# One more second product by two Strassen levels in a fused attention and expert kernel

## The chip, the cores and the metric

The kernel runs on one core of one Trainium2 chip. The metric is device time in microseconds (us) of one execution; smaller is better. The core has a matrix engine (TensorE, PE in the profile), three engines for elementwise work (VectorE or DVE, ScalarE or ACT, GpSimd or POOL), and a queue engine (SyncE, SP) that issues nearly all DMA transfers here. Every engine works through its own instructions in order and waits on semaphores for the others. PEld is TensorE's weight load, which overlaps its matmuls.

## The reference

First comes a linear attention with decay over blocks of 64 tokens (4 batches, 8 heads, 768 tokens, head size 64). Its output, brought to 3072 rows of 512, is the input `x` of four expert networks, whose results are added with normalised weights:

```python
x = np.ascontiguousarray(attn_out.transpose(0, 2, 1, 3)).reshape(B * S, H * D)   # 3072 x 512
p = domain_probs / (domain_probs.sum(-1, keepdims=True) + 1e-09)
for e in range(4):
    h = np.maximum(x @ w1[e], 0.0)          # 512 x 1024
    out += p[:, e:e + 1] * (h @ w2[e])      # 1024 x 512
```

Everything is float32. In this document `x @ w1[e]` is the first product and `h @ w2[e]` the second one.

## The kernel before, in words

The 3072 tokens are cut into three groups g of 1024. A pair (g, e) of a group and an expert is a unit; there are twelve, numbered 0 to 11 in the order in which they are worked. Strassen's scheme replaces the eight products of 2x2 blocks by seven, at the price of sums of blocks before and after. The first products of units 1 to 11 use it on two levels (7 x 7 block products). The second products of groups 0 and 1 (units 0 to 7) use it on one level: seven products `M1` to `M7`, each made of sixteen 128x128x256 matmuls (`second_product`, matmuls at L1028). Those of group 2 (units 8 to 11) use two levels: 7 x 7 products of two such matmuls each (`nested_product`, L1256). So a one-level second product costs 112 matmuls and a two-level one 98. The profile records each of these float32 matmuls as two instructions. The last unit has a few special forms (`plain_product`, `turned_product`).

The second product of unit u and the first product of unit u+1 are interleaved by the main loop: seven products, each in eight slots. After every slot the loop advances its own clock `now[0]` by one and hands out other work: queued VectorE sums (`background`), GpSimd steps (`aside`), the attention of the next groups, and `pump`, which starts larger GpSimd jobs from the list `chores` and the DMA stores from `queue` by due times. Those due times come from a rough cost model in the same units (`busy` for GpSimd, `filled` for VectorE, `free` for when the next chore may begin). In each engine the instructions stand in the order that this gives.

One-level form. The hidden blocks are turned into operand sums by VectorE (`operands`, `later_operands`), tokens are the rows of the result, and `scalar_tensor_tensor` at L1046 multiplies with the token's gate and adds into eight `acc` tiles, which SP stores straight to the output after expert 3.

Two-level form. GpSimd first multiplies the hidden blocks with the gates (`gated`, with `gate_bc`, which lies in the `decay` tile of the attention), VectorE and ScalarE make the outer sums T1 to T4 (`outer_sums`: ScalarE copies one operand to PSUM as `hp` at L838, VectorE writes `hT`), GpSimd makes the inner sums into `acc` tiles (`inner_sums`), and the results pile up in seven `sums` tiles in which the rows are output columns and the columns are tokens. They are added over the four experts and turned only once, at the end. The `sums` tiles take all seven buffers of the pool `stage`.

The two-level form needs each w2 block split into seven operands (S and A blocks) in DRAM, `w2_ops`. `prepare_w2_ops(e)` makes them on GpSimd, one expert in each of units 4 to 7; it needs `stage` buffers too, and every operand set is written by six DMA stores. `feed3` reads them back as `w2t`, four loads for each product. `feed` loads w1 operands as `ws_in` with two buffers, each one product ahead. `x_fill` loads the x blocks of a group, and `x_inner` makes four differences from each of the seven on GpSimd (`xs`).

Line L102 is the helper `tt` through which all elementwise sums go, so the rows of the profile have to be told apart by tile names.

Of the kernel before, what the change touches and what calls it, by code (L numbers as in the profile page):

```python
# [21 lines left out]
def kernel(  # L22
# [78 lines left out]
    def tt(eng, o, a, b, op):  # L101
        eng.tensor_tensor(out=o, in0=a, in1=b, op=op)  # L102
        if eng is nc.gpsimd:
            busy[0] = max(busy[0], now[0]) + math.prod(o.shape[1:]) / 480
        else:
            vector(math.prod(o.shape[1:]), PSUM in (a.space, b.space))
# [6 lines left out]
    now, busy, free, filled = [0], [0.0], [0.0], [0.0]  # L113
# [7 lines left out]
    LAST = NG - 1  # L121

# [47 lines left out]
    def store(f):  # L170
        queue.append((busy[0] + 2, f))
# [7 lines left out]
    def pump(pace=1.0, force=False):  # L179
        all_added(None if force else now[0])  # L180
        while results:
            results.pop(0)()
        while late and (force or late[0][0] <= now[0]):
            late.pop(0)[1]()
        begins = chores and (force or free[0] <= now[0])
        while queue and (force or queue[0][0] <= now[0] or begins and len(queue) > LEFT):
            queue.pop(0)[1]()
        if begins:
            begin = free[0] = max(free[0], now[0] - 1)
            was = max(busy[0], now[0])  # L190
            chores.pop(0)()
            free[0] = max(free[0], begin + max(pace * (busy[0] - was), 1))
# [106 lines left out]
    def inner_w2(e, m, blk):  # L299
        b = {f"A{i + 1}{j + 1}": blk[:, j, :, i * P:(i + 1) * P] for i in range(2) for j in range(2)}  # L300
        s = stage.tile([P, 4, 2, P], FP32, name="ops", tag="st")
        for name, x, y, op in S_OPS:
            b[name] = s[:, SLOT[name]]
            tt(nc.gpsimd, b[name], b[x], b[y], op)
        to = w2_ops[e, MS.index(m)]
        store(lambda: (
            nc.sync.dma_start(out=to[:, 0], in_=b["A11"]),
            nc.sync.dma_start(out=to[:, 1:3], in_=s[:, 0:2]),
            nc.sync.dma_start(out=to[:, 3], in_=b["A22"]),
            nc.sync.dma_start(out=to[:, 4], in_=b["S1"]),  # L310
            nc.sync.dma_start(out=to[:, 5], in_=b["A12"]),
            nc.sync.dma_start(out=to[:, 6], in_=b["S4"]),
            made.add(("w2", e, m)),
        ))

    def prepare_w2_ops(e):
        st = {}

        def block(name, i, j):
            t = stage.tile([P, 2, 2, DH], FP32, name="w2b", tag="st")  # L320
            src = moe_w2[e, j * W:(j + 1) * W, i * DH:(i + 1) * DH]
            nc.sync.dma_start(out=t[:].rearrange("p q c d -> p (q c) d"), in_=src.rearrange("(k p) d -> p k d", p=P))
            st[name] = t

        def total(name, a, b, op):
            t = stage.tile([P, 2, 2, DH], FP32, name="w2o", tag="st")
            halves(*(x[:].rearrange("p q c d -> p q (c d)") for x in (t, st[a], st[b])), op)
            st[name] = t

        return weight_steps(block, total, lambda m: inner_w2(e, m, st[A_OF[m]]))  # L330
# [21 lines left out]
    def x_fill(g, m):  # L352
# [8 lines left out]
        chores.insert(0, lambda: x_inner(g, m))  # L361
# [133 lines left out]
    last_gate = consts.tile([P, CPG * E], FP32, name="last_gate")  # L495


    gate_rows = dram.tile([CPG, E, P], FP32, name="gate_rows")
    gate_bc = decay[:]

    def gates():
# [8 lines left out]
        for i in range(CPG):  # L510
            t = token(LAST, i // 4, i % 4) // P
            nc.vector.tensor_copy(out=last_gate[:, i * E:(i + 1) * E], in_=gate[:, t])

    def turn_gates():
        p, o = bank("s0", "gp"), small("gr")
        n = CPG * E
        nc.tensor.transpose(out=p[0:n, 0:P], in_=last_gate[:], identity=ident[:])
        nc.scalar.copy(out=o[0:n, 0:P], in_=p[0:n, 0:P])
        nc.scalar.dma_start(out=gate_rows[:].rearrange("n e p -> (n e) p"), in_=o[0:n, 0:P])
# [291 lines left out]
    outer = {e: {n: {} for n in ("B11", "B12", "B21", "B22", "T1", "T2", "T3", "T4")} for e in range(E)}  # L811
# [43 lines left out]
    EARLY = E - 1, "M3"  # L855
# [42 lines left out]
    def finished(g, e, m, blocks, new):  # L898

        def later(to, a, b, order, relu=False):  # L900
# [7 lines left out]
            def step(at):  # L908
                x = there[at]
                if g == LAST and at != order[-1]:  # L910
                    bring(order[order.index(at) + 1])
                o = to[at] if at in to else small("m" + at)
                tt(nc.vector, o[:], x[:], b[at][:], ALU.add)
                if relu:
                    nc.scalar.activation(out=o[:], in_=o[:], func=AF.Relu)  # L915
                    if g == LAST:
                        gated(e, 1, 1, at, o)
# [4 lines left out]
            if g == LAST:  # L922
# [3 lines left out]
        def keep(c, i, j):  # L926
            if g == LAST:
                outer_sums(e, *{(0, 1): (("T1",), ("T3", "T2")), (1, 0): (("T4",),)}.get((i, j), ()))
# [21 lines left out]
    def first_product(g, e, m, blocks, tags):  # L950
# [3 lines left out]
        while (g, e) == (0, 1) and to_do[m]:  # L954
# [12 lines left out]
        def inner(i):  # L967
# [17 lines left out]
            if m in OUT and (at == "12" or not begins):  # L985
                nc.scalar.activation(out=new[at][:], in_=new[at][:], func=AF.Relu)  # L986
                if g == LAST:
                    gated(e, *OUT[m], at, new[at])
# [24 lines left out]
    def second_product(g, e, m, banks):  # L1013

        def part(sj, s):
# [31 lines left out]
            if e == E - 1 and m in ("M2", "M6", "M5", "M3"):  # L1047
                results.append(lambda: nc.sync.dma_start(out=rows[n][:, j * DH:(j + 1) * DH], in_=o))
# [10 lines left out]

    SEQ3 = ("M1", "M3", "M5", "M7", "M6", "M2", "M4")  # L1060
# [3 lines left out]
    def feed3(e, m, k):  # L1064

        until(("w2", e, m))
        if e == E - 1 and m != SEQ3[0]:

            if k == 0:
                t = xp.tile([P, 7, 256], FP32, name="w2s", tag="x" + SEQ[SEQ3.index(m)])  # L1070
                if (e, m) == PLAIN:
                    i, j = int(A_OF[m][1]) - 1, int(A_OF[m][2]) - 1
                    src = moe_w2[e, j * W:(j + 1) * W, i * DH:(i + 1) * DH]
# [3 lines left out]
                nc.sync.dma_start(out=t[:], in_=w2_ops[e, MS.index(m)].rearrange("p k c d -> p k (c d)"))  # L1077
# [6 lines left out]
            out=t[:, 0:n], in_=w2_ops[e, MS.index(m), :, 2 * k:2 * k + n].rearrange("p k c d -> p k (c d)"),  # L1084
# [97 lines left out]
    PLAIN = E - 1, "M2"  # L1182
# [23 lines left out]
    END = E - 1, SEQ3[-1]  # L1206
# [28 lines left out]

    def nested_product(e, m, tags):
        if e == 0:
# [8 lines left out]
        def inner(x, i):  # L1246
# [16 lines left out]
            if begins and e == 0:  # L1263
# [7 lines left out]
        def done():  # L1271
            if e == E - 1:
                to_join(m)

# [13 lines left out]
    def own_x(m):  # L1288
# [3 lines left out]
        def sub(f):  # L1292
            def step():
                steps.pop()
                f()
                if not steps:
                    made.add(("x", 0, m))
# [3 lines left out]
        for f in x_steps(0, m, nc.vector):  # L1301
            sub(f)
        own_sums.extend(steps)
# [149 lines left out]
    units = [(g, e) for g in range(NG) for e in range(E)]  # L1453
    fill = [(*u, m) for u in units[2:] for m in SEQ]
    fill2 = [(*u, m) for u in units[:-E] for m in SEQ2]
# [51 lines left out]
    fill3 = [(e, m, k) for e in range(E) for m in SEQ3 for k in range(4)]  # L1507
# [6 lines left out]
    PACE = 1.0, 1.4, 1.0  # L1514
    for at, (g, e) in enumerate(units):
# [3 lines left out]
        nested, nests = g == LAST, ahead and ahead[0] == LAST  # L1519
        if g == LAST - 1:  # L1520
            chores.extend(prepare_w2_ops(e))
        if at == 6:
            forget()
        blocks, banks = {}, {}
        for i in range(7):
            if fill2:
                feed2(*fill2.pop(0))
            if (g, e) < (LAST, 0):
# [5 lines left out]
            if nests and i == 2:  # L1534
                nc.scalar.dma_start(
                    out=gate_bc, in_=gate_rows[:, ahead[1]].partition_broadcast(P),
                )
            if nested:
                pair = (at * 7 + i) % 2 if ahead else i % 3
                b = nested_product(e, SEQ3[i], (("q01", "q02"), ("q11", "q12"), ("g1", "g3"))[pair])  # L1540
                if i < 6 and (e, SEQ3[i + 1]) != PLAIN:
                    inner_sums(e, SEQ3[i + 1])
            else:
                b = second_product(g, e, SEQ2[i], banks)
            if nests and i == 6:
                inner_sums(ahead[1], SEQ3[0], nested)
                if ahead[1] == EARLY[0]:
# [4 lines left out]
            if nested and (e, SEQ3[i]) == END:  # L1552
# [9 lines left out]
            for x, part in enumerate(order):  # L1562
# [15 lines left out]
                if nested or nests:  # L1578
                    take(aside)
                if nested and ahead and x in (1, 3) and fill3:  # L1580
# [47 lines left out]
```

## Time and profile before

| | |
|---|---|
| median of 3 runs | 1175.31 us (1172.42 to 1177.07) |
| the profiled execution, its own time | 1171.55 us |
| its span, from first to last instruction | 1169.8 us |
| TensorE busy | 1157.8 us, 99% of the span |
| VectorE, GpSimd, ScalarE busy | 791.7, 646.1, 271.1 us |
| moved by DMA | 255.63 MB |
| unit 7: from its first second-product matmul to that of unit 8 | 772.77 to 864.73 us |
| unit 8: the same | 864.73 to 949.41 us |

A row of the groups names the line, engine and operation, then "out<-in" by tile names, the shapes, "xcount", the busy time with the mean of one in ns, and last the idle time of the engine before these instructions with what ended it. A waits row reads "engine, line, waited for: total us, times, longest". A row of the stretches gives, for a window, its length and for each engine the busy us and the number of instructions, then the granted TensorE clock, the DMA share and GB/s. A timeline row has start, length, engine, line, operation and count.

### The profile page before, as it was taken

The numbers are of one execution on the slowest core, as the hardware profiler recorded it, in microseconds if no ns is written. First come the engines' busy times: TensorE is split into PE (matmuls) and PEld (weight loads), VectorE is DVE, ScalarE is ACT, GpSimd is POOL, SyncE is SP. The second block draws the span as 40 slices with busy tenths as digits, with TensorE's granted clock in tenths as the row PEclk, the third lists the DMA queues.
The fourth block names the chain that finished last, engine by engine and source line by source line (L and its number), as shares of the span: only waits on it lengthen the run. The fifth ranks groups of instructions, "written<-read, shape, count | busy, mean of one in ns | idle before, by whom it ended". The sixth has DMA issues, their size and how long they took to land.

```text
span 1169.8 us, 21185 instructions
## 1 busy us (share of the span) xinstructions
PE 1157.8 (99%) x8095; PEld 1006.5 (86%) x8095; DVE 791.7 (68%) x1407; ACT 271.1 (23%) x540; POOL 646.1 (55%) x640
## 2 busy tenths in 40 slices
PE   8999999999999999999999999999999999999998
PEld 7888888888888888888888888888888888888887
DVE  4666895578478567657747836745775666777785
ACT  4321122112211201211211120221233342341231
POOL 2846327546655761065245215655893683882884
PEclk9999999999999999999999999999999999999999
DMA  9884668998997996787868757785765445354442
GB/s 208 219 257 153 185 195 264 289 315 255 310 334 228 311 277 188 221 264 230 247 195 261 243 182 239 215 278 184 252 212 194 140 152 181 129 182 148 154 180 73
DMA packets 265717, 255.63 MB, mean 219 GB/s; under 512 B 121328, under 2 KB 219408, under 8 KB 265616
## 3 DMA queue, kind: packets, MB, share of 16 engines
q1 hardware_dynamic: 254976, 251.46, 69.0%
q10 hardware_dynamic: 10640, 2.82, 1.1%
q8 instruction: 64, 1.05, 0.4%
q14 instruction: 37, 0.30, 0.1%
HBM read 180.80 MB, written 77.61 MB: 221 GB/s over the span
## 4 chain that ended last, share of the span: by engine, by line
PE 95%; DVE 3%; POOL 1%; issue 0%; DMA 0%; ACTq 0%; ACT 0%; POOLq 0%; DVEq 0%
PE pg L974 39%; PE q L1028 31%; PE pq L1256 13%; PE pM L1358 2%; PE pc L1358 2%; DVE m L102 1%; PE sp L633 1%; PE op L687 1%; PE op L705 1%; PE sp L640 1%; PE qp L603 1%; PE kp L603 1%; POOL acc L102 1%; POOL m L102 1%; DVE sums L102 0%
## 5 line engine op out<-in xcount | busy, mean ns | idle before, releaser
L974 PE MATMUL pg<-xs,ws_in 128*128 128x256 f32 x1960 | 471.6, 380 | 0.8 <-DVE m L102 0.7
L1028 PE MATMUL q<-w2t,m 128*128 128x256 f32 x1792 | 424.4, 380 | 0.0
L974 PEld LDWEIGHTS pg<-xs,ws_in 128*128 128x128 f32 x1960 | 369.8, 190 | 53.7 <-DVE m L102 3.3
L102 DVE TENSOR_TENSOR m<-pg,m 128x512 f32<-128x512 f32 x451 | 307.2, 687 | 120.0 <-PE pg L974 109.8
L1028 PEld LDWEIGHTS q<-w2t,m 128*128 128x128 f32 x1792 | 339.3, 190 | 46.6 <-DVE m L102 0.4
L1046 DVE SCALAR_TENSOR_TENSOR acc<-q,gate,acc 128x256 f32<-128x256 f32 x192 | 92.3, 481 | 126.2 <-PE q L1028 125.7
L102 DVE TENSOR_TENSOR m<-m,m 128x512 f32<-128x512 f32 x184 | 152.5, 829 | 7.7 <-ACT m L986 7.7
L986 ACT ACTIVATE m<-m 128x512 f32<-128x512 f32 x132 | 83.0, 630 | 303.6 <-DVE m L102 302.5
L102 POOL TENSOR_TENSOR m<-m,decay 128x512 f32<-128x512 f32 x64 | 81.8, 1293 | 58.1 <-ACT m L986 44.7
L102 DVE TENSOR_TENSOR sums<-pq,sums 128x256 f32<-128x256 f32 x153 | 64.1, 421 | 45.7 <-PE pq L1256 36.9
L982 ACT COPY m<-pg 128x512 f32<-128x512 f32 x88 | 51.5, 585 | 186.1 <-PE pg L974 176.1
L1256 PE MATMUL pq<-acc,w2t 128*128 128x256 f32 x352 | 86.6, 379 | 0.0
L102 POOL TENSOR_TENSOR xs<-xs 128x256 f32<-128x256 f32 x56 | 44.5, 794 | 73.1 <-DMA xs<-x_blocks 57.4
L1256 PEld LDWEIGHTS pq<-acc,w2t 128*128 128x128 f32 x352 | 66.8, 190 | 9.3 <-issue 0.3
L102 POOL TENSOR_TENSOR to<-xc 128x256 f32<-128x256 f32 x16 | 12.5, 783 | 95.8 <-DVE xc L102 67.8
L102 POOL TENSOR_TENSOR acc<-hT,hT 128x512 f32<-128x512 f32 x32 | 40.2, 1269 | 29.7 <-PE pq L1256 27.8
L102 POOL TENSOR_TENSOR kn<-kn,decay 128x512 f32<-128x512 f32 x16 | 18.0, 1123 | 64.6 <-PE kp L603 43.7
L102 POOL TENSOR_TENSOR w2o<-w2b 128x512 f32<-128x512 f32 x32 | 42.4, 1348 | 18.3 <-DMA w2b<-in_moe_w_dram 10.2
L915 ACT ACTIVATE m<-m 128x512 f32<-128x512 f32 x44 | 27.7, 630 | 106.8 <-DVE m L102 106.8
L102 POOL TENSOR_TENSOR ops<-w2b 128x256 f32<-128x256 f32 x24 | 17.8, 764 | 50.7 <-issue 28.2
L102 POOL TENSOR_TENSOR acc<-hT,acc 128x512 f32<-128x512 f32 x32 | 40.7, 1271 | 7.4 <-PE pq L1256 5.4
L102 POOL TENSOR_TENSOR w2o<-w2b,w2o 128x512 f32<-128x512 f32 x24 | 34.2, 1449 | 5.8 <-issue 4.3
(135 smaller groups left out, 1204.8 us busy)
## 6 DMA issues: line engine op xcount, KB each, us to landing
ws_in<-w_ops SPq DMA_DIRECT2D x70, 896.0 KB, 6.3
w2t<-w_ops SPq DMA_DIRECT2D x66, 256.0 KB, 5.1
w2t<-w_sums SPq DMA_DIRECT2D x64, 256.0 KB, 3.7
w_ops<-ops SPq DMA_DIRECT2D x28, 512.0 KB, 4.3
w2t<-in_moe_w_dram SPq DMA_DIRECT2D x48, 256.0 KB, 3.6
w2b<-in_moe_w_dram SPq DMA_DIRECT2D x32, 256.0 KB, 5.5
w_sums<-w2o SPq DMA_DIRECT2D x16, 512.0 KB, 5.7
w2b<-in_moe_w_dram SPq DMA_DIRECT2D x16, 512.0 KB, 7.6
```

Of the source, the lines that this page charges most:

```text
L102: eng.tensor_tensor(out=o, in0=a, in1=b, op=op)
L603: nc.tensor.transpose(out=x[:, ac * C:(ac + 1) * C], in_=y[:, 2 * ac:2 * ac + 2].rearrange("p r d -> p (r d)"), identity=ident[:],)
L633: nc.tensor.matmul(out=sp[r][half[x], ac * BL:(ac + 1) * BL], lhsT=hc(kT)[half[r], ac, blk[x]], rhs=hc(qT)[half[r], ac, blk[x]], start=(ac ...
L640: nc.tensor.matmul(out=sp[x][half[r], 256 + ac * D:256 + (ac + 1) * D], lhsT=kd[half[x], 2 * ac + r], rhs=vn[half[x], 4 * r + ac], start=F ...
L915: nc.scalar.activation(out=o[:], in_=o[:], func=AF.Relu)
L974: nc.tensor.matmul(out=p[:, j * 256:(j + 1) * 256], lhsT=ws[i][:, j * P:(j + 1) * P], rhs=xs[i], start=(fresh and j == 0), stop=True, skip ...
L982: nc.scalar.copy(out=new[at][:], in_=p[:])
L986: nc.scalar.activation(out=new[at][:], in_=new[at][:], func=AF.Relu)
L1028: nc.tensor.matmul(out=p[:, s * DH:(s + 1) * DH], lhsT=h[A_OF[m]][:, c * 256 + s * P:c * 256 + (s + 1) * P], rhs=fed2[g, e, m][uu][:, c], ...
L1046: nc.vector.scalar_tensor_tensor(out=o, in0=x, scalar=w, in1=o, op0=ALU.mult, op1=ALU.add)
L1256: nc.tensor.matmul(out=p[:, 0:256], lhsT=fed3[e, m, x // 2][:, x % 2, c * P:(c + 1) * P], rhs=b[B_OF[i]][:, c * 256:(c + 1) * 256], start= ...
L1358: nc.tensor.matmul(out=p[:, s * 256:(s + 1) * 256], lhsT=a[c][:, f:f + P], rhs=b[:, c, j * 256:(j + 1) * 256], start=(s == 0 and c == 0 an ...
```

## The change

Unit 7, which is group 1 with expert 3, now makes its second product in the two-level form. What goes with it:

- The last group works its experts in the order 3, 0, 1, 2; units 7 and 8 both read the w2 operands of expert 3.
- The operands of experts 3, 0 and 1 are queued together at unit 4 (`PREPARED`); those of expert 2 are made from unit 7 on, with tiles of the general pool, since the seven `stage` buffers now hold `sums` from unit 7 on. From then on (`spare`) GpSimd chores start at least 8 slots apart and only when GpSimd is modelled as free, and stores fall due 8 slots after the modelled end.
- Experts 0 to 2 of group 1 still end in `acc` tiles, which are stored to a DRAM tile `partial` in unit 6. The two-level result of unit 7 is joined by VectorE and GpSimd (`first_done`), parked in DRAM (`parked`, columns by tokens), gathered in eight tiles of 128 tokens as 32x32 blocks (four DMAs each), turned by VectorE's 32x32 transpose, added to `partial` by GpSimd and stored.
- For four of the seven x blocks of group 2 the four differences go to VectorE.
- The gates of group 1 are turned as well, and `gate_bc` is written from unit 6 on.

```diff
-            busy[0] = max(busy[0], now[0]) + math.prod(o.shape[1:]) / 480
+            busy[0] = max(busy[0], now[0]) + math.prod(o.shape[1:]) / (640 if spare else 480)
...
+    units = [(g, e) for g in range(NG) for e in ((3, 0, 1, 2) if g == LAST else range(E))]
+    unit_of = {u: x for x, u in enumerate(units)}
+    NEST = 2 * E - 1
+    FINAL = len(units) - 1
...
-        queue.append((busy[0] + 2, f))
+        queue.append((busy[0] + (8 if spare else 2), f))
...
-        begins = chores and (force or free[0] <= now[0])
+        begins = chores and (force or free[0] <= now[0] and not (spare and busy[0] > now[0] + 1))
...
-            free[0] = max(free[0], begin + max(pace * (busy[0] - was), 1))
+            free[0] = max(free[0], begin + max(pace * (busy[0] - was), 8 if spare else 1))
...
+        return [
+            lambda: (block("A21", 1, 0), block("A22", 1, 1)), pause(6),
+            lambda: total("S1", "A21", "A22", ALU.add),
+            lambda: (ready("M4"), block("A11", 0, 0), drop("A22")), pause(4),
+            less, lambda: ready("M7"), lambda: (ready("M1"), drop("S3")), lambda: ready("M5"),
+            lambda: (total("S2", "S1", "A11", ALU.subtract), block("A12", 0, 1)), lambda: ready("M6"),
+            lambda: ready("M2"),
+            lambda: total("S4", "A12", "S2", ALU.subtract), lambda: ready("M3"),
+        ]
...
-        chores.insert(0, lambda: x_inner(g, m))
+        if g == LAST and SEQ.index(m) >= 3:
+            own_x(m, g, 6)
+        else:
+            chores.insert(0, lambda: x_inner(g, m))
...
-        for i in range(CPG):
-            t = token(LAST, i // 4, i % 4) // P
+        for i in range(LAST * CPG):
+            t = token(1 + i // CPG, i % CPG // 4, i % 4) // P
             nc.vector.tensor_copy(out=last_gate[:, i * E:(i + 1) * E], in_=gate[:, t])
...
-            if e == E - 1 and m in ("M2", "M6", "M5", "M3"):
-                results.append(lambda: nc.sync.dma_start(out=rows[n][:, j * DH:(j + 1) * DH], in_=o))
+            if unit_of[g, e] in (E - 1, NEST - 1) and m in ("M2", "M6", "M5", "M3"):
+                to = rows[n] if g == 0 else partial[n % CPG * P:(n % CPG + 1) * P]
+                results.append(lambda: nc.sync.dma_start(out=to[:, j * DH:(j + 1) * DH], in_=o))
...
+    def first_done(m):
...
+        def park(x):
+            i, j = RESULT[x]
+            to = parked[i * DH:(i + 1) * DH, j * W:(j + 1) * W].rearrange("(k p) t -> p k t", k=2)
+            of_x = of[x]
+            store(lambda: nc.sync.dma_start(out=to, in_=of_x[:].rearrange("p (k t) c -> p k (t c)", k=2)))
+
+        def gather(n):
+            t, po = small("y"), small("po")
+            for b in range(4):
+                c = n * P + b * 32
+                nc.sync.dma_start(
+                    out=t[b * 32:(b + 1) * 32].rearrange("p (r c) -> p r c", c=32),
+                    in_=parked[:, c:c + 32].rearrange("(r p) c -> p r c", p=32),
+                )
+            nc.sync.dma_start(out=po[:], in_=partial[n * P:(n + 1) * P])
+            gathered_out[n] = t, po
+
+        def turn_rows(n):
+            t = gathered_out[n][0]
+            nc.vector.transpose(out=t[:], in_=t[:])
+            vector(W, False)
+
+        def finish_rows(n):
+            t, po = gathered_out.pop(n)
+            tt(nc.gpsimd, t[:], t[:], po[:], ALU.add)
+            store(lambda: nc.sync.dma_start(out=rows[CPG + n], in_=t[:]))
...
+        if m == "M5":
+            for k in range(2):
+                then(1, ("M3", "M5"), lambda k=k: plus("M3", "M5", k, nc.gpsimd))
+        if m == "M6":
+            for a, b in (("M6", "M1"), ("M3", "M6"), ("M7", "M6"), ("M5", "M7")):
+                for k in range(2):
+                    then(1, (a, b), lambda a=a, b=b, k=k: plus(a, b, k))
+                if a in ("M3", "M5"):
+                    then(1, (a,), lambda a=a: park(a))
+        if m == "M2":
+            for k in range(2):
+                then(1, ("M1", "M2"), lambda k=k: plus("M2", "M1", k))
+            then(1, ("M2",), lambda: park("M2"))
+        if m == "M4":
+            for k in range(2):
+                then(1, ("M4", "M7"), lambda k=k: plus("M4", "M7", k))
+            then(1, ("M4",), lambda: park("M4"))
+            order = 4, 5, 6, 7, 0, 1, 2, 3
+            for n in order:
+                then(6, (), lambda n=n: gather(n))
+                then(6, (), lambda n=n: turn_rows(n))
+                then(2, (), lambda n=n: finish_rows(n))
...
-        if e == 0:
+        if e in (NEST, 2 * E):
+            while any(m in of for of, *_ in ending):
+                end_first(True)
             sums[m] = stage.tile([P, 4, 256], FP32, name="sums", tag="st")
...
-    fill2 = [(*u, m) for u in units[:-E] for m in SEQ2]
+    fill2 = [(*u, m) for u in units[:NEST] for m in SEQ2]
...
+    PREPARED = {NEST - 3: (3, 0, 1), NEST: (2,)}
...
-        nested, nests = g == LAST, ahead and ahead[0] == LAST
-        if g == LAST - 1:
-            chores.extend(prepare_w2_ops(e))
+        nested, nests = at >= NEST, ahead and at + 1 >= NEST
+        if at in PREPARED:
+            for x in PREPARED[at]:
+                chores.extend(prepare_w2_ops(x, nested))
+        if at == NEST:
+            spare.append(True)
...
+                    if own_sums and fits():
+                        take(own_sums)
+                if ending and fits():
+                    end_first()
```

## The prediction

> **What bounds the kernel now.** I read the page first (shares, groups), then the PE timeline for the true pace, then the stretches of single units, then the waits.
>
> ```profile
> span 1169.8 us, 21185 instructions
> PE 1157.8 (99%) x8095; PEld 1006.5 (86%) x8095; DVE 791.7 (68%) x1407; ACT 271.1 (23%) x540; POOL 646.1 (55%) x640
> ...
> L974 PE MATMUL pg<-xs,ws_in 128*128 128x256 f32 x1960 | 471.6, 380 | 0.8 <-DVE m L102 0.7
> L1028 PE MATMUL q<-w2t,m 128*128 128x256 f32 x1792 | 424.4, 380 | 0.0
> ```
>
> TensorE is busy 99% of the span, and before its two large groups it sat idle 0.8 and 0.0 us. So the number of matmuls sets the time, and other engines matter only where they would make TensorE wait. The 380 ns are not the pace, because matmuls overlap; the timeline has it:
>
> ```profile
> 772.77 1.89 PE L1028 MATMUL q<-w2t,m 128*128 128x256 f32 x8
> 774.50 1.89 PE L974 MATMUL pg<-xs,ws_in 128*128 128x256 f32 x8
> 776.22 1.89 PE L1028 MATMUL q<-w2t,m 128*128 128x256 f32 x8
> ```
>
> From start to start 16 records take 3.45 us: 215.7 ns each, and 215.9 over longer stretches. A matmul is two records, 0.432 us. The stretches of units 6 to 10:
>
> ```profile
> 682.00:772.80 90.80, 90.80 (x422) 79.75 (x421) 58.36 (x93) 14.74 (x24) 51.77 (x60) 1.00 0.73 230
> 772.80:864.70 91.90, 91.32 (x421) 79.42 (x420) 59.03 (x93) 21.17 (x36) 59.20 (x59) 1.00 0.74 239
> 864.70:949.40 84.70, 84.67 (x392) 74.58 (x393) 50.65 (x86) 33.58 (x72) 56.56 (x46) 1.00 0.49 165
> 949.40:1034.10 84.70, 84.70 (x394) 74.41 (x393) 61.73 (x114) 25.57 (x46) 55.29 (x45) 1.00 0.46 159
> ```
>
> A one-level unit has 420 records (90.7 us by the pace), a two-level one 392 (84.6 us). Unit 7 (second row) takes 1.3 us more than its records. The reason is a chain that starts on POOL:
>
> ```profile
> ACT hp L838 <- POOL m L102: 7.2, 1, 7.2
> ```
>
> ScalarE's first `hp` copy waited for a gated block, VectorE's `hT` behind it stood 1.97 us, and TensorE lost some 0.5 us, then another 0.67 us at the first two-level matmul, whose bank VectorE freed late. This is how a late GpSimd reaches TensorE.
>
> **The change, part by part.**
>
> *TensorE.* 14 matmuls fewer (112 to 98): 28 records x 215.9 ns = 6.05 us, all on the path. The transpose of the gates grows from 32 to 64 columns once, nothing.
>
> *VectorE* (rows: `acc` 481 ns, `m<-m,m` 829, `sums<-pq` 421, `hT` 681, `m<-up` 680, `xs` 653, transpose of 128x512 700). Removed: 28 `acc` steps (13.5 us) and 24 `m<-m,m` (19.9). Added: 21 `sums` additions (8.8), 16 `hT` (10.9), 8 `m<-up` (5.4), 12 joins of `sums` of which two operands lie in SBUF (taken as `m<-m,m`, 9.9), 16 `xs` differences (10.4), 8 transposes (5.6). Net +17.6 us over units 6 to 10, where the engine has 23 to 34 us free in each unit of 85 to 92; by the order of instructions unit 7 gets the most, about 66 us of work in 84.6. Hidden, so nothing, as long as no single lump is longer than what TensorE tolerates: by the timeline a bank is written again about 2.6 us after its last block ended, which leaves VectorE 1.9 us beside the 0.69 of its addition. The longest lump is three joins in a row at the start of unit 8 (2.5 us): I allow 0.3 us. The gates of group 1 add eight copies of 128x4 near 69 us (eight took 0.66 us); VectorE idles 1.04 us just after, so nothing.
>
> [...] `m<-m,m` takes 829 ns and single ones up to 1.45 us, against 687 with one operand in PSUM. [...] By the rows, which were taken beside a GpSimd 60 to 70% busy, unit 7 stays at 66. I take the rows.
>
> *GpSimd.* +54 sums of 128x512 (16 gate multiplications, 28 inner sums, 2 joins, 8 final additions; 1.27 us each, 68.6) and 16 `xs` fewer (x 0.79 = 12.7): +55.9 us. The w2 operands (28 small sums at about 0.79 and 8 at about 1.35, 33 us an expert) stay the same work but leave unit 6 and fill units 4 and 5; expert 2's fall into units 7 to 9. By order unit 8 then holds 43 gate and inner sums (54.6), two final additions (2.5), 20 small and 2 large operand sums (18.5): 75.6 of 84.6 us, after 56.6 before. Unit 9 holds 73, unit 10 52. So it is no bound on average, but 90% busy in order. Who waits? First TensorE for inner sums:
>
> ```profile
> 940.50 2.50 POOL L102 TENSOR_TENSOR acc<-m,m 128x512 f32<-128x512 f32 x2
> 943.09 2.63 POOL L102 TENSOR_TENSOR acc<-m,acc 128x512 f32<-128x512 f32 x2
> ...
> 952.93 1.89 PE L1256 MATMUL pq<-acc,w2t 128*128 128x256 f32 x8
> ```
>
> The last of these four ends at 945.72 and is first read at 953.79, 8.1 us later, which is the least margin in units 8 to 10. A chore ahead of it (4 small sums, 3.2 us) and a final addition (1.3) leave 3.6. Second, the `hp` copies, with almost no margin: adding up GpSimd's work in order puts five gated blocks some 2.4 to 3.4 us behind the place of the copy; the case above was about 6 us late and cost 0.5 us. I take 0.1 us each, 0.5 in all; at unit 7's old price it is 2.5.
>
> *ScalarE.* +28 copies of 128x256 (368 ns) and 20 of 128x512 (588): 22 us on an engine that is 23% busy. Nothing.
>
> *SP and DMA.* 82 issues more: 32 gathers, 8 loads of `partial`, 8 stores of rows, 4 of `parked`, the rest from operands that now come in halves. Moved: the stores to `partial` and the three operand sets pass SP one to three units sooner. Queued behind each are the next `w2t` and `ws_in`. The margins from landing to first use in units 8 to 10: `w2t` 3.6 us at the least and 6.5 as a rule, `ws_in` 6 to 9. SP runs ahead and then stands for TensorE:
>
> ```profile
> SPq L887 <- PE pg L974: 124.6, 19, 6.6
> ```
>
> That is 6.6 us in nearly every product of 12.1 us, room for ten issues of 0.6. A tile's gather is 2048 pieces of 128 bytes. No row has it; the nearest is `across`, 256 such pieces, 5.1 us to landing (2.1 to 9.9). A packet takes 50.6 ns of a DMA engine on average (69.0% of 16 x 1169.8 us over 254976 packets), so 2048 on 16 engines take 6.5 us, plus 2.1: some 9 us, at the upper end 8 x 3.0 + 2.1 = 26. The transpose stands at least 6 slots (9.1 us) behind, and SP issues ahead of its place. I take nothing, at 26 us it is rival three. Stores of GpSimd's results now come 8 slots later, so SP waits less for them.
>
> *Gone again:* unit 7's 1.3 us. The same first gating now lies in unit 6, where GpSimd has 44 instructions after 62 in the old place. I count two thirds, 0.9.
>
> **The sum.** -6.05 - 0.9 + 0.3 + 0.5 = -6.1 us. Span 1169.8 to 1163.7; the profiled execution, 1.75 us longer than its span, 1171.55 to 1165.4. It lies 3.8 us below the median of the runs, so the same step from the median gives 1169.2. A measurement of this kernel tells about 0.5% (5.9 us) from no change: the forecast lies just past that line, at 0.52%.
>
> **The rivals.**
>
> 1. *GpSimd falls behind.* For it: 90% in unit 8, the five late blocks, and its own model counts a small sum as 0.4 slots (0.6 us) where the rows have 0.79. Against: 8 us of margin on the inner sums. If each of the five costs 0.5 us and each two-level unit once meets a late inner sum (1 us for 3 units), +5 instead of +0.5: about 1172.5 (1170.5 to 1175).
>
> 2. *More than the matmuls is won.* All of unit 7's 1.3 us goes and nothing new comes: -7.3, 1168.0.
>
> 3. *The gathers hold up the weights: slower.* If eight gathers keep the DMA engines near the 26 us, the next `w2t` lands late by what exceeds 6.5 us of margin and the 9 us above. It decides from about 17 us a tile on; at 18.5 each of eight tiles costs 1.5 to 2 us, 12 to 16 in all: 1182. [...] Against: the DMA engines are only 46 to 50% busy in these units, and the 6.5 us from the packet's mean is taken from a mix with 121328 packets under 512 bytes.
>
> That the change does not do what it says can be left out: built, it has 2462 matmuls of 128x256 instead of 2476.
>
> **How the numbers follow.** The forecast with its own range of 1167 to 1170.8: 0.52; rival 2, 0.12; rival 1, 0.28; rival 3, 0.08. Faster by over 0.5% (under 1169.4): 0.38 of the first, 0.11 of rival 2 and 0.06 of rival 1, 0.55. Slower: rival 3 and a tail of rival 1, 0.08. The same: 0.37. The range reaches from rival 2's place less a us of scatter to the top of rival 1: 1166.8 to 1175.
>
> **What would show it.** Unit 7's stretch falls from 91.95 to about 84.8 us, units 8 to 10 stay at 84.7 to 85.5. GpSimd reaches about 75 us in unit 8. The `hp` copies show five or so waits for POOL of 2 to 4 us. The gathers land in 6 to 12 us. Wrong would be: units 8 to 10 over 86 us with TensorE idle before L1366 (inner sums, `w2t`), or transposes of `y` that wait for DMA with TensorE idle after them.

## The result

The changed kernel takes 1168.35 us in the median of 22 runs (1167.22 to 1175.77), the kernel before, over as many runs, 1175.83 us (1169.76 to 1183.16). The ratio of the means is 0.9945 with a 95% interval of 0.9928 to 0.9961: 0.55% faster, forecast 0.52%. The total came out as forecast; several of the terms in it did not, as the units show.

The page of the changed kernel, the lines that answer to those of before:

```profile
span 1169.7 us, 21473 instructions
PE 1155.8 (99%) x8067; PEld 1004.1 (86%) x8067; DVE 808.3 (69%) x1444; ACT 290.6 (25%) x588; POOL 702.8 (60%) x678
...
L1009 PE MATMUL pg<-xs,ws_in 128*128 128x256 f32 x1960 | 471.8, 381 | 1.2 <-DVE m L102 1.1
...
L1063 PE MATMUL q<-w2t,m 128*128 128x256 f32 x1568 | 371.3, 380 | 0.0
...
L1366 PE MATMUL pq<-acc,w2t 128*128 128x256 f32 x464 | 114.2, 379 | 0.6 <-DMA w2t<-w_ops 0.6
```

The group of one-level matmuls has lost 224 records, a unit's worth, and the largest two-level group now has an idle time of its own, 0.6 us before `w2t`. The span is the same as before, 1169.7 us, and that says nothing of the change: in this profile the part before unit 0 took 91.58 us, in that of before 86.40. From unit 0's first second-product matmul to the end it is 1078.13 us after 1083.36. The stretches of units 5 to 9, with the boundaries taken from this trace (columns as in the stretches of before):

```profile
590.70:687.20 96.50, 96.07 (x645) 83.47 (x645) 65.94 (x109) 16.23 (x32) 56.51 (x60) 1.00 0.76 239
687.20:777.90 90.70, 90.70 (x421) 79.71 (x420) 60.20 (x96) 21.04 (x36) 48.52 (x46) 1.00 0.69 218
777.90:862.90 85.00, 84.94 (x393) 74.23 (x392) 63.96 (x106) 33.08 (x71) 67.64 (x54) 1.00 0.60 200
862.90:949.20 86.30, 85.35 (x393) 74.22 (x392) 57.16 (x94) 34.62 (x74) 74.96 (x69) 1.00 0.83 254
949.20:1033.90 84.70, 84.70 (x393) 74.41 (x393) 63.28 (x117) 25.57 (x46) 64.77 (x54) 1.00 0.66 205
```

Unit 7 (third row) went from 91.96 to 85.0 us, as forecast, and no engine beside TensorE is full: GpSimd does 74.96 us of work in unit 8, forecast 75.6. But unit 8 costs 86.3 instead of 84.7, and unit 5 96.5 instead of 95.8. In unit 8 TensorE's timeline (start, length, instruction; in brackets the wait before it) says why:

```profile
907.28 1.10 PE L1366 MATMUL pq<-acc,w2t 128*128 128x256 f32 x4 [0.56 <-DMA w2t<-w_ops]
...
912.87 1.13 PE L1366 MATMUL pq<-hT,w2t 128*128 128x256 f32 x4 [0.18 <-DMA w2t<-w_ops]
```

By the starts of the matmuls the two waits cost 0.80 and 0.44 us. SP's own timeline of the 17 us before shows what the weights stood behind:

```profile
890.02 5.75 SPq L1300 DMA_DIRECT2D y<-parked  x4
898.52 0.34 SPq L1304 DMA_DIRECT2D po<-partial  x1
898.91 0.43 SPq L312 DMA_DIRECT2D w_ops<-w2o  x1
...
902.26 0.93 SPq L330 DMA_DIRECT2D w2b<-in_moe_w_dram  x2
903.28 0.89 SPq L1121 DMA_DIRECT2D w2t<-w_ops  x2
```

The first gathered tile held SP from 890.0 to 898.9 (its last load stood 2.7 us for the load of the gates, `decay<-gate_rows`), then came six operand stores and two loads, and only then the `w2t` for which TensorE stood at 907: it landed 3.9 us after its issue, and TensorE started 0.1 us later. The third of that set landed 8.1 us after its issue, and TensorE started on it at once.

### The profile page after: what moved, and what is told of

Its sections match the earlier page's. It is cut to its first block, busy times and chain, and to the rows that moved or that the text cites. A ratio compares the mean times of both kernels' runs of the same rounds, so it can differ in the third digit from the quotient of the medians.

```text
span 1169.7 us, 21473 instructions
## 1 busy us (share of the span) xinstructions
PE 1155.8 (99%) x8067; PEld 1004.1 (86%) x8067; DVE 808.3 (69%) x1444; ACT 290.6 (25%) x588; POOL 702.8 (60%) x678
## 3 DMA queue, kind: packets, MB, share of 16 engines
q8 instruction: 64, 1.05, 0.4%
## 4 chain that ended last, share of the span: by engine, by line
PE 94%; DVE 3%; DMA 1%; issue 1%; ACT 0%; ACTq 0%; SPq 0%; DVEq 0%
PE pg L1009 39%; PE q L1063 28%; PE pq L1366 16%; PE pM L1470 3%; DVE m L102 2%; PE pc L1470 2%; PE sp L668 1%; PE op L722 1%; PE op L740 1%; PE sp L675 1%; DVE sums L102 1%; DMA w2t<-w_ops 1%; PE kp L638 1%; PE qp L638 1%; DMA kn<-in_k_dram 0%
## 5 line engine op out<-in xcount | busy, mean ns | idle before, releaser
L1063 PE MATMUL q<-w2t,m 128*128 128x256 f32 x1568 | 371.3, 380 | 0.0
L1063 PEld LDWEIGHTS q<-w2t,m 128*128 128x128 f32 x1568 | 296.8, 190 | 40.6 <-DVE m L102 0.2
L1081 DVE SCALAR_TENSOR_TENSOR acc<-q,gate,acc 128x256 f32<-128x256 f32 x164 | 78.9, 481 | 102.7 <-PE q L1063 102.1
L102 DVE TENSOR_TENSOR m<-m,m 128x512 f32<-128x512 f32 x160 | 133.7, 835 | 6.3 <-ACT m L1021 6.3
L102 POOL TENSOR_TENSOR m<-m,decay 128x512 f32<-128x512 f32 x80 | 103.5, 1313 | 53.2 <-ACT m L1021 35.5
L1366 PE MATMUL pq<-acc,w2t 128*128 128x256 f32 x464 | 114.2, 379 | 0.6 <-DMA w2t<-w_ops 0.6
L1366 PEld LDWEIGHTS pq<-acc,w2t 128*128 128x128 f32 x464 | 88.0, 190 | 13.1 <-issue 1.2
L102 POOL TENSOR_TENSOR xs<-xs 128x256 f32<-128x256 f32 x40 | 32.0, 799 | 58.7 <-DMA xs<-x_blocks 56.3
L1366 PE MATMUL pq<-hT,w2t 128*128 128x256 f32 x192 | 49.4, 380 | 0.2 <-DMA w2t<-w_ops 0.2
L873 ACT COPY hp<-m 128x512 f32<-128x512 f32 x60 | 34.7, 589 | 32.4 <-DVE hT L102 18.9
```

What stands on the lines that cost most here:

```text
L873: nc.scalar.copy(out=there[x][:], in_=blk[at][:])
L1063: nc.tensor.matmul(out=p[:, s * DH:(s + 1) * DH], lhsT=h[A_OF[m]][:, c * 256 + s * P:c * 256 + (s + 1) * P], rhs=fed2[g, e, m][uu][:, c], ...
L1081: nc.vector.scalar_tensor_tensor(out=o, in0=x, scalar=w, in1=o, op0=ALU.mult, op1=ALU.add)
L1366: nc.tensor.matmul(out=p[:, 0:256], lhsT=fed3[e, m, x // 2][:, x % 2, c * P:(c + 1) * P], rhs=b[B_OF[i]][:, c * 256:(c + 1) * 256], start= ...
```

## The experiments

All stretches are from one profile of each kernel, unit by unit as above. Units 3 and 4 took 95.79 and 98.48 us in every one of them except the last one, with unit 6 changed too, so a stretch can be read to some hundredths of a us where nothing else changed; the times of whole runs can't.

| kernel | unit 5 | unit 6 | unit 7 | unit 8 | units 9, 10 | unit 11 | 5 to 11 |
|---|---|---|---|---|---|---|---|
| before | 95.78 | 90.75 | 91.96 | 84.68 | 169.55 | 50.81 | 583.5 |
| changed | 96.47 | 90.69 | 85.01 | 86.33 | 169.55 | 50.92 | 579.0 |
| changed, again | 96.48 | 90.68 | 85.00 | 86.09 | 169.54 | 50.92 | 578.7 |
| before, 14 matmuls fewer | 95.78 | 90.95 | 87.21 | 84.68 | 169.55 | 50.82 | 579.0 |
| the same, operands at unit 4 | 96.48 | 90.75 | 86.15 | 84.61 | 169.54 | 51.19 | 578.7 |
| x differences on GpSimd | 96.46 | 96.74 | 88.09 | 85.28 | 169.55 | 50.91 | 587.0 |
| the same, begun later | 96.47 | 91.42 | 86.21 | 85.28 | 169.60 | 50.92 | 579.9 |
| operands one expert a unit | 95.78 | 96.40 | 85.77 | 85.27 | 169.55 | 50.92 | 583.7 |
| chores and stores not spaced | 96.47 | 90.67 | 96.80 | 85.88 | 169.54 | 50.91 | 590.3 |
| no gathers | 96.47 | 90.68 | 85.03 | 85.09 | 169.55 | 50.93 | 577.8 |
| expert 2's operands later | 96.46 | 90.68 | 85.57 | 85.29 | 170.62 | 50.92 | 579.5 |
| gathers two slots apart | 96.48 | 90.67 | 85.01 | 85.09 | 169.54 | 53.12 | 579.9 |
| gathers one slot apart | 96.47 | 90.69 | 85.01 | 85.09 | 169.54 | 50.92 | 577.7 |

The theories: A, the matmuls set the time and the rest is hidden but for a us or two; B, GpSimd's order reaches TensorE; C, SP's order does. What each forecasts is said anew in each expectation, and a rival there can be another one.

### The matmuls alone

```diff
                 for c in range(2):
+                    if (g, e, s, uu, c) == (1, 3, 0, 1, 1):
+                        continue
                     nc.tensor.matmul(
```

> The kernel before, with 14 of the 112 matmuls of unit 7's second product left out (the last of every second group of four) and nothing else touched; part of the sum for unit 7's result is missing. It prices the matmuls alone. Theory A (the matmuls set the time): unit 7's stretch falls from 91.96 to about 85.9 us (28 records x 215.9 ns = 6.05), ratio about 0.995, the same as the change gives; all that the change adds is then hidden or cancels. Rival B (TensorE is not the only bound there, GpSimd's chain holds unit 7): the stretch falls by less than 5 us, and the change won something beside the matmuls.

Measured: unit 7 at 87.21 us, 4.75 less instead of 6.05; ratio 0.9969 (0.9953 to 0.9984). B is nearer: of the 6.05 us that the matmuls are worth, 1.3 went into waits, which doubled in unit 7 to 2.6 us. Half of them, 1.4 us by the starts of the matmuls, lie behind the late gating by GpSimd (again 7.2 us of wait before the first `hp`, at 863.3); the other half lie before it, from 854.9 to 859.3, where TensorE waited for VectorE. So the change got 6.95 us from unit 7 because something else moved too. Which part it was:

```diff
-        if g == LAST - 1:
-            chores.extend(prepare_w2_ops(e))
+        if at == E:
+            for x in range(E):
+                chores.extend(prepare_w2_ops(x))
```

> The kernel before with the same 14 matmuls of unit 7 left out as in the first experiment (part of that sum is missing) and, in addition, the w2 operands of all four experts queued at unit 4 instead of one expert in each of units 4 to 7. There the matmuls alone gave 87.2 us in unit 7. If the rest of what the change won in unit 7 came from taking the operand sums out of the way of the first gating: unit 7 at 84.7 to 85.5 us. If it came from the x differences on VectorE instead: unit 7 stays above 86.5.

Measured: unit 7 at 86.15 us, 5.81 less than before: between the two expectations. In ScalarE's waits around unit 7, the row below (us in all, number, longest), the wait of `hp` for GpSimd fell from 7.2 to 4.5 us, and TensorE no longer lost anything behind it; taking the operand sums away from the gating brought 1.06 of the 2.2 us. What is left, some 1.5 us from 848.9 to 855.0, are the waits for VectorE before the first `hp`; why the changed kernel has only 0.3 us of them was not tested. Unit 5 went up by 0.70 us, exactly as in the changed kernel: that is the price of operands made earlier. The ratio is 0.9968 (0.9952 to 0.9984).

```profile
ACT hp L838 <- POOL m L102: 4.5, 1, 4.5
```

### The three parts that make room on GpSimd, undone one at a time

x differences on GpSimd again:

```diff
-        if g == LAST and SEQ.index(m) >= 3:
+        if False:
```

> The changed kernel with all x differences of group 2 on GpSimd again (16 more there of 0.79 us, 16 fewer on VectorE). Theory A (hidden on either engine): units 6 and 7 stay within 0.5 us of 96.5-less-5.8 = 90.7 and 85.0, the total within 1 us of the changed kernel. Rival B (GpSimd's lateness reaches TensorE through the hp copies): units 6 and 7 together rise by 1 to 3 us, the waits of hp for POOL grow from 13.4 us.

Measured: unit 6 at 96.74 and unit 7 at 88.09 us, 8.1 us lost in units 6 to 8, more than all of the gain; the ratio is 1.0019 (1.0004 to 1.0034), slightly slower than before. Theory A falls for this part and B named the way but was three times too small: units 6 and 7 together rose by 9.1 us, and 1.05 of that came back in unit 8, since this kernel has no wait for `w2t` there. ScalarE's waits in units 6 and 7 of this kernel:

```profile
ACT hp L873 <- POOL m L102: 12.3, 1, 12.3
```

and GpSimd's own in the same stretch:

```profile
POOL xs L102 <- DMA xs<-x_blocks: 28.1, 4, 12.2
```

The first `hp` waited 12.3 us (6.2 in the changed kernel, where unit 6 loses nothing by it). Most of the standing for x loads is not new: the same row of the changed kernel reads 24.7 us in two waits. What counts is where it falls. The chain that ended last in this kernel (start, length, what), from an x load to the matmuls of TensorE:

```profile
755.06 3.71 DMA xs<-x_blocks
...
759.22 0.74 POOL xs L102
...
763.38 5.41 POOL m L102 x4
...
776.40 0.60 ACT hp L873
...
777.03 0.69 DVE hT L102
...
778.37 2.07 PE pg L1009 x4
```

GpSimd stood 4.0 us before this block of differences and then worked 4.2 us on them, with the gate multiplications for the `hp` copies behind. Is it the place in line or the work?

```diff
-            own_x(m, g, 6)
+            late.append((now[0] + 7, lambda: x_inner(g, m)))
```

> The changed kernel with the four x blocks back on GpSimd, as in the run with all x differences there (unit 6 at 96.7, unit 7 at 88.1 us), but each begun 7 slots (10.6 us) after its loads are issued and not at once. If that loss came from GpSimd standing for the x loads with the gate multiplications behind it (28.1 us in four waits there): unit 6 falls to 90.7 to 91.5 and unit 7 to 85.0 to 86.5. If it came from the 12.7 us of work itself: unit 6 stays above 94 us.

Measured: unit 6 at 91.42, unit 7 at 86.21 us, as expected of the first cause. In units 6 and 7 it loses 1.9 us against the changed kernel, not 9.1 (over units 6 to 8 it is 0.9, not 8.1); `hp` waits 7.2 us. The same 16 sums on the same engine, begun later, cost a fifth: it was their place in line, not the work. How much of the rest was standing idle and how much were sums that came too early, this does not separate. The ratio is 0.9957 (0.9940 to 0.9974).

Operands one expert a unit, as before:

```diff
-    PREPARED = {NEST - 3: (3, 0, 1), NEST: (2,)}
+    PREPARED = {NEST - 3: (3,), NEST - 2: (0,), NEST - 1: (1,), NEST: (2,)}
```

> The changed kernel with the w2 operands of experts 3, 0, 1 made in units 4, 5, 6, one in each, as in the kernel before, instead of all three from unit 4 on. Theory A: only the first gating in unit 6 meets a busier GpSimd, as it did in unit 7 before, where it cost 1.3 us: unit 6 rises from 90.7 to 91.0 to 92.0, and the 0.7 us that unit 5 lost to VectorE goes; in all 0 to 1 us more. Rival B: operands that need stage buffers run into unit 7, whose sums need the same buffers: unit 7 rises by 2 us or more.

Measured: unit 6 at 96.40, unit 7 at 85.77 us, unit 5 back at 95.78; over units 5 to 11 nothing is left of the gain, the ratio is 0.9985 (0.9965 to 1.0005). Again one long wait at the first gating, in ScalarE's waits:

```profile
ACT hp L873 <- POOL m L102: 11.6, 1, 11.6
```

Theory A was right on the place, but unit 6 rose by 5.7 us where it had at most 1.3. Unit 7 rose by 0.8 us, and that is not trouble with `stage`: its first four records took 1.62 us from start to start, where the pace gives 0.86, behind the long wait (see the last section), which is the 0.8 us.

No spacing:

```diff
-        if at == NEST:
-            spare.append(True)
```

> The changed kernel without the spacing of GpSimd chores and stores from unit 7 on. Expert 2's operands (33 us) then run in unit 7 almost without a pause, and stores fall due sooner, so SP meets unfinished GpSimd work. Theory A with the margins of the prediction (8 us on inner sums, hardly any on hp): unit 7 rises by 1 to 4 us through hp waits and late stores ahead of w2t. If GpSimd's order does not matter at all: unit 7 stays at 85.0. Rival B: unit 7 rises by 5 us or more, and the change would lose its gain.

Measured: unit 7 at 96.80 us, 11.8 more, ratio 1.0035 (1.0018 to 1.0053). That is rival B. GpSimd did 87.9 us of work in unit 7, and here even the inner sums came too late, which nowhere else happened (TensorE's timeline of this kernel):

```profile
855.25 1.13 PE L1366 MATMUL pq<-acc,w2t 128*128 128x256 f32 x4 [3.50 <-POOL acc L102]
856.59 2.08 PE L1366 MATMUL pq<-acc,w2t 128*128 128x256 f32 x4 [0.21 <-POOL acc L102]
...
867.30 2.08 PE L1366 MATMUL pq<-hT,w2t 128*128 128x256 f32 x4 [2.84 <-DVE sums L102]
```

### The late weights in unit 8

Without gathers, transposes, final additions and stores of the gathered rows:

```diff
             order = 4, 5, 6, 7, 0, 1, 2, 3
-            for n in order:
-                then(6, (), lambda n=n: gather(n))
-                then(6, (), lambda n=n: turn_rows(n))
-                then(2, (), lambda n=n: finish_rows(n))
```

> The changed kernel without the eight gathers, transposes, final additions and row stores of group 1's result (those rows are not written). Theory C (the two waits for w2t in unit 8, 1.2 us, come from SP issuing the first gather ahead of the operand stores and the weight loads): unit 8 falls from 86.3 to about 85.0 us and TensorE waits for no w2t; units 9 and 10 stay at 84.7 to 84.9. Rival B (GpSimd's load in unit 8 is the cause): unit 8 stays within 0.3 us of 86.3. The total is 1 to 1.5 us below the changed kernel by C.

Measured: unit 8 at 85.09 us and no wait for `w2t`; the rest unchanged; ratio 0.9926 (0.9900 to 0.9953). C holds: the 1.24 us come from the gathers. Is it their place in SP's order or their traffic? Counted from the start of unit 8, the first of the awaited loads was issued at 38.4 us here and at 40.4 in the changed kernel, and took 3.9 us to landing in both: that wait is SP's order alone. The third took 7.5 us here and 8.1 there, so of the 2.6 us by which it came later 0.7 are a slower transfer. The 1.24 us are also all that gathering and turning the result costs.

```diff
-    PREPARED = {NEST - 3: (3, 0, 1), NEST: (2,)}
+    PREPARED = {NEST - 3: (3, 0, 1), NEST + 1: (2,)}
```

> The changed kernel with the w2 operands of expert 2 begun at unit 8 instead of unit 7, so their first stores come after the first gathers. Theory C (gather and operand stores together, not the gather alone): the w2t waits of unit 8 shrink to under 0.5 us, unit 8 at 84.9 to 85.6 us, and unit 9 may get some of it, up to 1 us. If the gather alone is the cause, unit 8 stays at 86.3. Rival B: unit 7 falls below 84.9 since GpSimd has fewer chores there, and unit 9 or 10 rises over 86.

Measured: unit 8 at 85.29 us, units 9 and 10 together 1.07 us longer, and unit 7 0.56 us longer instead of shorter, which no theory had. So the stores behind the gather are needed for the wait in unit 8, but moved they cost as much elsewhere: 579.5 us over units 5 to 11, ratio 0.9950 (0.9926 to 0.9975). How finely the two must meet is seen in the three kernels with unit 8 at 85.27 or 85.28 us: gathers and stores are all there, the first awaited load was issued 1.4 to 1.6 us sooner than in the changed kernel, and TensorE did not wait for it.

Gathers two slots apart:

```diff
-        def gather(n):
-            t, po = small("y"), small("po")
-            for b in range(4):
...
+        def gather(n, b):
+            if b == 0:
+                gathered_out[n] = small("y"), small("po")
+            t, po = gathered_out[n]
+            if b == 4:
+                nc.sync.dma_start(out=po[:], in_=partial[n * P:(n + 1) * P])
+                return
+            c = n * P + b * 32
...
-                then(6, (), lambda n=n: gather(n))
+                for b in range(5):
+                    then(2, (), lambda n=n, b=b: gather(n, b))
```

> The changed kernel with the five loads of each gathered tile issued two slots apart instead of at once. Theory C: SP is no longer held for 9 us in one piece, the w2t waits go or fall under 0.4 us, unit 8 at 84.9 to 85.5 us, the total 1 us below the changed kernel, ratio to before about 0.9935. If what counts is the number of issues and not their being together, unit 8 stays at 86 or more. The group of eight tiles takes longer, but ends before the last unit, so its end costs nothing.

Measured: unit 8 at 85.09 us, as expected, but unit 11 at 53.12, 2.2 us more, and the ratio is 0.9963 (0.9948 to 0.9978). Eight tiles of 18 slots instead of 14 no longer end before the last unit, against what I had written. In the chain that ended last a gathered tile stands ahead of VectorE's work in the last unit (first row), and TensorE then waited for VectorE (second row); its last matmul ended 1.45 us later in the unit. The other 0.75 us are SP's: its last issue of the whole program was a row of the gathered tiles, and its landing ended the span (third row, SP's timeline).

```profile
1119.27 9.71 DMA y<-parked
...
1131.64 2.83 PE L1369 MATMUL pq<-hT,w2s 128*128 128x256 f32 x12 [0.47 <-DVE sums L102]
...
1173.03 0.42 SPq L1317 DMA_DIRECT2D out_dram<-y  x1
```

One slot apart (against the version two slots apart):

```diff
-                    then(2, (), lambda n=n, b=b: gather(n, b))
-                then(6, (), lambda n=n: turn_rows(n))
+                    then(1, (), lambda n=n, b=b: gather(n, b))
+                then(5, (), lambda n=n: turn_rows(n))
```

> The changed kernel with the five loads of each gathered tile one slot apart, so that a tile takes 12 slots where it took 14 in the changed kernel and 18 in the version two slots apart. The last tile is then done before the last unit. Unit 8 at 85.1, the last unit at 50.9 (not 53.1), the part from unit 0 on 1.2 us shorter than in the changed kernel: about 1076.9 us; ratio 0.993 to 0.9945 to the kernel before. If the loads are again too close together, unit 8 stays at 86.3.

> The changed kernel once more, on the same chip as the version above. The units repeat within 0.3 us each (unit 7 at 85.0, unit 8 at 86.3), while the part before unit 0 differs by several us from profile to profile; the part from unit 0 on is again 1078.1 us.

Measured on the same chip: unit 8 at 85.09 against 86.09 us, unit 11 at 50.92 in both, units 5 to 11 at 577.7 against 578.7; ratio 0.9938 (0.9918 to 0.9958) against 0.9942 (0.9917 to 0.9967). The wait is gone and nothing came back for it, 1.0 us by the units; the times of the runs can't tell the two apart. From unit 0 on the profile shows 1078.8 us, not the expected 1076.9, and the repeated kernel 1077.2, since units 0 to 2, in which the two programs do the same, took 306.8 us in one and 304.2 in the other.

### One more unit

```diff
-    NEST = 2 * E - 1
+    NEST = 2 * E - 2
...
-    PREPARED = {NEST - 3: (3, 0, 1), NEST: (2,)}
+    PREPARED = {NEST - 3: (2, 3), NEST + 1: (0, 1)}
...
-    BEGIN = {1: (24, 13), 2: (8 * 19, 22)}
+    BEGIN = {1: (24, 13), 2: (8 * 17, 18)}
```

> The changed kernel with unit 6 in the two-level form as well (two Strassen levels for experts 2 and 3 of group 1), operands of experts 2 and 3 from unit 3 on, of 0 and 1 from unit 7 on, the attention of group 2 at 18 slots a block instead of 22 and begun 16 slots sooner. Theory A: another 6.05 us less from 14 matmuls, less 1 to 3 us of new waits in units 3 to 5 (denser attention) and 7 to 9 (GpSimd and SP): 1163 to 1166, ratio about 0.990. Rival B (GpSimd at 90% has no room for more): units 7 to 9 rise by 6 us or more in sum, no gain over the changed kernel.

Measured: 1209.15 us, ratio 1.0292 (1.0261 to 1.0324). Unit 6 did fall to 84.81 us, 5.9 less, so theory A holds for the matmuls. But unit 4 rose from 98.48 to 115.22 and units 9 and 10 from 169.55 to 194.65: TensorE waited 9.72 us at once for a `w2t` in unit 10 and 7.37 for VectorE in unit 9. In unit 4 one wait of 8.73 us stands before a matmul of the attention, which the trace puts down to GpSimd's operand sums (`w2o`), so the denser attention and the earlier operands are both in it. Unit 3 rose by 5.8 us, and unit 5 fell by 4.8. The loss in units 9 and 10 comes with operands of two experts made while the two-level units run; which of the edits costs what was not separated.

## Why the prediction was right, and where not

- *14 matmuls are 6.05 us*: right as a price; unit 6 in the last experiment gave 5.9 as well. But only where GpSimd and VectorE are out of the way: alone they gave 4.75.
- *Two thirds of unit 7's 1.3 us go, 0.9*: too little. All of it went: in unit 6, where the first gating now lies, `hp` waited 6.2 us and TensorE lost nothing. That unit 7 fell by just 0.90 more than the matmuls is chance, since VectorE's new waits at its end took 0.3 back.
- *VectorE's lumps 0.3, late `hp` copies 0.5*: TensorE waited for VectorE at the end of unit 7 (0.22 + 0.10) and at the start of unit 8 (0.37 + 0.10), 0.8 in all. The `hp` copies waited for GpSimd once at the end of unit 6 and three times in units 7 to 10, 13.4 us together, without a cost that can be seen. One term too small by 0.5, the other too large by 0.5: that the sum fits is luck.
- *VectorE at 66 us in unit 7, by the rows*: it needed 64.0; `m<-m,m` takes 835 ns in the mean of the whole kernel, after 829. For the total of a unit the rows were a good guide; but the mean hides what a sum takes at one place (next point but one).
- *"I take nothing" for SP and DMA*: this step failed. It measured 1.24 us. I had counted room for ten issues of 0.6 us a product and margins of 6.5 us, and had not put the first gather and the operand stores behind each other, though both stand before the same `w2t`. The gather itself was priced about right: a tile took 4.3 to 10.0 us from its first issue to its last landing (one of its four loads 5.6 in the median), where I had estimated some 9 and at most 26. Rival three had the right victim at a tenth of its price, but another mechanism: it had the transfers hold the weights up, and they were issued late.
- *Operands "leave unit 6 and fill units 4 and 5"*, for nothing: they cost 0.7 us in unit 5, seen with them in the kernel before as well and gone without them. TensorE waited there for VectorE, whose sums had grown slower beside GpSimd's, 1008 ns in the mean after 708 (last section).
- Together: -6.95 in unit 7, +1.65 in unit 8, +0.69 in unit 5 and +0.11 at the end give -4.6 us from the traces (-4.8 in the repeated one), against -6.1. The ratio's interval, -4.6 to -8.5 us, just holds that. Whether the rest is chance or lies before unit 3 can't be told: there the profiles of like work spread over ten us. That the forecast of the total fits so well is partly luck.
- *Rival one* got 0.28 on the ground that GpSimd is 90% busy. What decides is not its load alone but how long the first gate multiplications stand behind other work. The prediction did see that chain, but priced the edits that shorten it (x on VectorE, operands sooner, spacing) as costs to be hidden. Undone, each takes back 8.1, 4.7 (with unit 5's 0.7 counted in its favour) and 11.3 us.

## What to carry to other kernels

Where one engine is full, price what it saves first, but look in the trace for the in-order engine whose late step reaches it, and treat every edit that moves work on that engine as part of the gain. On an engine that works in order, a step that is placed before it can run costs what stands behind it; here beginning it later saved 7.2 of the 9.1 us lost in units 6 and 7, and giving it to an engine with room all of them. And a mean duration hides what an instruction takes at the place where the engine beside it is busy: 835 ns over the kernel, 1008 in 22 us of unit 5. For a queue that issues DMAs, list what stands ahead of the next needed load at each place; an average room of so many issues does not show two bursts that meet, here 1.24 us in unit 8.

## What the runs showed of the hardware

Some long waits of TensorE cost more than themselves here. With the x differences on GpSimd it stood 4.93 us, and the granted clock of the stretches behind it (the third column from the end, after GpSimd's count, reads 0.50) shows the rest:

```profile
770.00:778.00 8.00, 3.44 (x16) 2.68 (x15) 2.06 (x4) 2.26 (x4) 7.69 (x9) 0.96 0.16 50
778.00:780.00 2.00, 1.63 (x4) 1.36 (x5) 1.90 (x4) 1.65 (x3) 1.92 (x3) 0.50 0.10 33
780.00:782.00 2.00, 2.00 (x7) 1.55 (x6) 1.90 (x4) 1.16 (x3) 2.00 (x3) 0.50 0.38 101
782.00:784.50 2.50, 2.50 (x8) 2.02 (x7) 0.58 (x1) 0.80 (x3) 2.50 (x3) 0.55 0.78 255
784.50:788.00 3.50, 3.50 (x18) 3.09 (x17) 0.35 (x2) 1.96 (x4) 3.34 (x3) 1.00 0.92 316
```

For some six us matmuls ran at half pace, nearly 3 us on top of the 5. With operands one expert a unit a wait of 4.53 us had the like behind it: the next eight records took 3.49 us from start to start, where the pace gives 1.73. The waits of 0.2 to 0.6 us in units 5 to 8 of the changed kernel had no such tail (granted clock 1.00 in each of these units), which is why a little less room on GpSimd turned from free into 6 us. But the length of a single wait does not settle it. Without the spacing one of 2.84 us, some 9 us after one of 3.50, was followed by half pace too: twelve records in 5.28 us instead of 2.59. And at 15.0 us, after the same matmuls, a wait of 2.31 us ended in the kernel before and one of 2.30 in the changed kernel; from 15 to 17 and from 17 to 20 us the granted clock was 1.00 and 1.00 in the first, 0.76 and 0.59 in the second. What else decides, these traces do not show.

VectorE's sums of two tiles in SBUF were slower beside a busy GpSimd. The rows are from the same 22 us of unit 5, in which GpSimd works 3.6 us in the kernel before (first row) and 14.5 us in the changed one (second row):

```profile
L102 DVE TENSOR_TENSOR m<-m,m 128x512 f32<-128x512 f32 x11 | 7.8, 708 | 0.0
L102 DVE TENSOR_TENSOR m<-m,m 128x512 f32<-128x512 f32 x10 | 10.1, 1008 | 0.0
```

A sum took 1008 ns in the mean after 708. With operands one expert a unit (GpSimd 4.9 us) it is 715 and the 0.7 us of unit 5 are gone; with 14 matmuls fewer and the operands at unit 4 (14.6 us) it is 1008 and they are there. What holds the sums up, the traces do not show.

The part before unit 0, in which the kernels here do nearly the same work, took from 86.4 to 96.9 us in these profiles; in all but the last kernel units 0 to 2 scatter by 1.0 to 1.4 us each, and units 3 and 4 repeat to 0.01 us. In the profile of the changed kernel the granted clock was 0.91 from 0 to 20 and from 40 to 60 us, in that of before 1.00. The clock is not all of it: with expert 2's operands later it was 1.00 throughout, and the part took 91.3 us. So the profiles differ mainly at the start; that the runs, which spread over 8 to 13 us, do so too is likely but not shown. An edit of 1 us late in the program is seen in stretches of the trace long before it is seen in times.
